# Expert rows turned by a transposing DMA instead of TensorE, a packed value projection, and a new planned order, in a kernel of attention and two mixtures

## The chip, the cores and the metric

The kernel runs on one core of a Trainium2 chip. The metric is device time in microseconds; the kernel before takes 529.66 us, the median of 3 runs (524.53 to 529.88). All engines of the core are named as in the profile: PE is TensorE, DVE is VectorE, ACT is ScalarE, POOL is GpSimd, SP is SyncE, whose only work here is to issue transfers.

## What is computed

Three stages follow each other, cut here to what matters:

```python
# 1: attention, 4 batches, 8 heads, 576 tokens, head size 64; heads 0-3 see the last 32 keys, heads 4-7 every fourth of 128
attn = softmax(where(mask, q @ k.T / 8, -1e9)) @ v
# 2: a mixture of 4 attention experts over x (4, 576, 512): all four are computed, the two best are kept
logits = x @ w_gate
y[e] = softmax(causal((x @ wq[e]) @ (x @ wk[e]).T / 8)) @ (x @ wv[e]) @ wo[e]
x2 = sum of w[kk] * y[topk[kk]]
# 3: a mixture of 8 feed-forward experts; each of the 2304 tokens goes to one expert
e = argmax(logits2) if s == 0 or local_gate < 0.5 else the expert of the token before
out = p[e] * (relu(x2 @ w1[e]) @ w2[e])       # w1: 512 x 1024, w2: 1024 x 512
```

The third stage is worked in float16 pairs: a value is kept as a high and a low part, and a product is the sum of high x high, high x low and low x high.

## The kernel before

The program has two parts.

**The planned part** holds the first two stages, the routing and three early slots of the third. Its instructions are recorded (class `Plan`), and `order` puts them in one order for each engine. It takes the instruction with the largest key that can start, where the key is the length of the chain behind the instruction, plus a number from the table `OFF` for the unit that it belongs to. So `OFF` sets the order. Its first units are these:

- `warm` filler matmuls (120, of `wn` = 256 columns) that write the tile Y from a tile of zeros. They have the lowest key and stand where PE has nothing else.
- `front` and `p1_stream`: the attention of eight pairs of heads (i = 0 to 7, two a batch). For a pair `p1_load` loads k and q, `p1_q` (POOL, ACT) lays q out, `p1_s` makes scores (PE, writes S) and their maximum (DVE), `p1_sub` and `p1_nrm` subtract and divide (POOL) around an exponential (ACT), `p1_t` transposes (PE, writes T) and `p1_pv` multiplies by v (PE, writes X and A). q is loaded into the tile of that pair's v, of which there are two, and v is loaded over it later by `p1_loadv`.
- `proj(b)`: the projections of batch b. q and k come first (matmuls of 288 columns into A), then v and the gate (line 417, as everything that is recorded): for each block of 128 tokens 12 matmuls of 260 columns, 256 for v and 4 for the gate. The fifth block has only 64 tokens and takes 12 matmuls too.
- `attn_stream`, `out_proj`, `route`, `early`, `slots`: the second stage's attention, its output, and the lists by which tokens go to experts.

**The slots.** The third stage works on groups of 128 tokens of one expert. `for t in range(NE, STATIC): slot(t, ...)` runs 18 of them in fixed program order, a conditional one follows; three early ones are in the planned part. One slot t is:

- SP: `w_load(t + 1)` (line 1237) issues eight loads of 512 KB into the staging tile `stg`, which are skipped where the expert stays the same. Each waits until DVE has split the chunk that lay there. SP's instructions stand in program order, so SP runs ahead of the engines by about a slot.
- POOL: `x_gather(t + 2)` (line 1266) gathers 128 rows of x2 by index from DRAM into one of `xgb` = 3 buffers, two slots ahead. At the slot's end `x_out(t)` (line 1312) scatters the 128 result rows. A buffer comes free when the slot's last ScalarE instruction (line 1309) has read its scale from it.
- ACT and DVE: eight `w_split` (lines 1257 and 1258) make the next slot's weights into high and low parts.
- PE: `mm1` twice (48 matmuls of 128 columns each, lines 1291 to 1293), then `x_t(t + 1)` (eight transposes of 128 x 128, line 1277, which ACT copies from PSUM, line 1279), then `mm2` (24 matmuls of 512 columns, lines 1303 to 1305).

Of the kernel before, what the change touches and what calls it, by code (L numbers as in the profile page):

```python
# [21 lines left out]
NB = 18  # L22
# [9 lines left out]
OFF = (20338.85, -10835.23, -17409.01, -12864.95, -10987.6, -10593.49, -17890.54, -11899.78, 22686.67, -19177.35,  # L32
# [27 lines left out]
KN = {"x0": (0, 1), "qk": (0, 1), "v2": (0, 1), "x2": (1, 1), "yt": (0, 1), "w": (0, 1), "f32t": 3,  # L60
      "early": 3, "pfl": (100000,), "wn": 256, "xp": "XA", "warm": 120, "off": OFF,
      "xgb": 3, "x2b": 3, "hx": "X", "hy": "A", "h2": "X", "fc": (0, 4),
      "banks": {"S": 2, "T": 2, "A": 2, "X": 1, "Y": 1}, "share": 32040, "emax": 22992,
# [95 lines left out]
class Plan:  # L159
# [96 lines left out]
    def price(eng, name, out, ins, a, k):  # L256
# [3 lines left out]
        if eng == "T":  # L260
            src = ins[-1] if name == "matmul" else ins[0]
            big = (src.proto if isinstance(src, View) else src).dtype == F32
            if sh[0] == 64 and n in (32, 64, 256, 288) and name == "matmul":
                return n / 2.4e3 * (2 if big else 0.5) + 0.003
# [175 lines left out]
def tile_attention_moe_moe(ctx: ExitStack, tc, qd, kd, vw, wqk, wvg, wo, woT, wg9, w1, w2,  # L440
# [77 lines left out]
    vh_w = wpool.tile([128, 4, 260], F16, name="wv_h")  # L518
    vl_w = wpool.tile([128, 4, 260], F16, name="wv_l")
    LDS, SPL, SVL, SE, TT, XP = {}, {}, {}, {}, {}, {}  # L520
    XH, XL = {}, {}

    S1 = [ld.tile([128, NB, 64], F32, name=f"s1{z}", bufs=1) for z in range(KN["bs"])]
    for y in S1:
        V.memset(y[:, :, 0:1], 1e-9)
    QZ = [ld.tile([128, 2 * NB, 64], F32, name=f"ldq{z}", bufs=1) for z in range(KN["bq"])]
    for z, y in enumerate(QZ):
        for h in range(2):
            (V if z else P).memset(y[64 * h:64 * h + 64, :, 32 - 32 * h:64 - 32 * h], 0.0)

    def p1_load(i):
        b, m = divmod(i, 2)
# [785 lines left out]
    def slot(t, hh, hl):  # L1318
# [15 lines left out]
        if nx:  # L1334
            x_t(t + 1)
# [174 lines left out]
```

## Time and profile before

| | |
|---|---|
| runs, us | 529.88, 529.66, 524.53 (median 529.66) |
| the profiled execution | 525.19 us, its span 523.3 us |
| PE, DVE, ACT, POOL busy in the span | 497.1, 427.2, 367.0, 137.0 us |
| planned part | 0 to 303.5 us |
| slots | 303.5 to 514 us, 19 of them |
| granted TensorE clock, mean | 0.987 of full speed |

Busy time is the time in which at least one instruction of an engine was under way; matmuls overlap, so the step from one start to the next is what a matmul costs its engine. The 9.3 us behind 514 us hold the last scatter and the program's end.

### The profile page before, as it was taken

What the parts mean: (1) busy time and instruction counts of PE and PEld (TensorE: products, weight loads), DVE (VectorE), ACT (ScalarE), POOL (GpSimd) and SP (SyncE); (2) the same over time, 40 slices, a digit from 0 to 9 for tenths busy, and PEclk for the clock granted to TensorE, in tenths of its full rate; (3) what the DMA queues carried; (4) which work ended last, traced back from release to release, by engine and by line L of the source; (5) the groups of instructions that cost most, each with busy time, mean ns of one, the idle gap of its engine ahead of it and who ended that gap; (6) DMA issues with size and microseconds to landing.
All of it is one profiled execution on the core that took longest, in us unless ns stands there. A gap on an engine that the chain in (4) does not pass through costs nothing.

```text
span 523.3 us, 17303 instructions
## 1 busy us (share of the span) xinstructions
PE 497.1 (95%) x6794; PEld 382.1 (73%) x6794; DVE 427.2 (82%) x1221; ACT 367.0 (70%) x620; POOL 137.0 (26%) x169
## 2 busy tenths in 40 slices
PE   7899999998999999989799999999999999999992
PEld 5787888887887887756577667777677776677760
DVE  4857558877988877899797169999999999999993
ACT  3454436664668657486482279999999999999992
POOL 7748233013321001131300211421112211123111
PEclk9999989999999999999999999999999999999997
DMA  8749777253203012312751826592165199561210
GB/s 310 277 135 283 223 221 208 60 195 118 67 25 72 26 46 64 90 70 55 254 210 53 320 104 211 189 329 86 42 212 192 49 358 381 175 216 60 63 43 15
DMA packets 33047, 79.89 MB, mean 153 GB/s; under 512 B 7486, under 2 KB 16190, under 8 KB 31936
## 3 DMA queue, kind: packets, MB, share of 16 engines
q1 hardware_dynamic: 29280, 67.70, 38.9%
q0 software_dynamic: 3680, 11.03, 6.1%
q8 instruction: 55, 0.90, 0.7%
q14 instruction: 32, 0.26, 0.2%
HBM read 112.52 MB, written 10.49 MB: 235 GB/s over the span
## 4 chain that ended last, share of the span: by engine, by line
DMA 20%; issue 19%; PE 11%; DVE 2%; POOL 0%; ACT 0%; POOLq 0%; another core or an unknown queue 0%
DMA out_dram<-o,SIDX 19%; PE A L417 3%; PE X L417 3%; DMA share<-x2d,GIDX 2%; PE T L417 1%; PE Y L417 1%; DVE s L417 1%; DVE tl L417 1%; DVE share L417 0%; PE S L1291 0%; PE S L1293 0%; PE S L1292 0%; PE A L1305 0%; PE A L1303 0%; PE A L1304 0%
## 5 line engine op out<-in xcount | busy, mean ns | idle before, releaser
L1258 DVE SCALAR_TENSOR_TENSOR share<-share 128x1024 f16<-128x1024 f32 x152 | 177.4, 1219 | 15.5 <-ACT share L1257 15.3
L1257 ACT ACTIVATE share<-share 128x1024 f16<-128x1024 f32 x152 | 149.7, 1048 | 0.2 <-DMA share<-in_w_dram 0.2
L417 PEld LDWEIGHTS <-share 128*128 128x128 f16 (+1 forms) x1430 | 116.9, 100 | 40.2 <-issue 4.2
L1293 PE MATMUL S<-share 128*128 128x128 f16 x608 | 102.8, 219 | 0.0
L1292 PE MATMUL S<-share 128*128 128x128 f16 x608 | 102.8, 219 | 0.0
L1291 PE MATMUL S<-share 128*128 128x128 f16 x608 | 102.8, 219 | 0.0
L417 PE MATMUL A<-share 128*128 128x288 f16 (+3 forms) x768 | 89.8, 270 | 0.7 <-DVE share L417 0.4
L1312 POOL DMA_INDIRECT out_dram<-o,SIDX x19 | 26.8, 1411 | 155.2 <-ACT o L1309 147.0
L1292 PEld LDWEIGHTS <-share 128*128 128x128 f16 x608 | 59.4, 98 | 2.3
L1291 PEld LDWEIGHTS <-share 128*128 128x128 f16 x608 | 59.5, 98 | 2.3
L1293 PEld LDWEIGHTS <-share 128*128 128x128 f16 x608 | 59.5, 98 | 0.0
L1303 PE MATMUL A<-share 128*128 128x512 f16 x152 | 57.8, 380 | 0.0
L1305 PE MATMUL A<-share 128*128 128x512 f16 x152 | 57.5, 378 | 0.0
L1304 PE MATMUL A<-share 128*128 128x512 f16 x152 | 57.5, 378 | 0.0
L417 ACT ACTIVATE th<-T 128x512 f16<-128x512 f32 (+3 forms) x84 | 42.0, 514 | 16.8 <-PE T L417 14.5
L417 ACT ACTIVATE s<-s,mx 128x256 f32<-128x256 f32 (+4 forms) x72 | 40.6, 582 | 13.9 <-DVE mx L417 12.8
L417 ACT ACTIVATE share<-A 128x288 f16<-128x288 f32 (+3 forms) x65 | 29.6, 455 | 21.5 <-PE A L417 14.0
L417 DVE CUSTOM_DVE_ANT_0 s<-S,tri 128x256 f32<-128x256 f32 (+4 forms) x80 | 37.1, 476 | 5.2 <-PE S L417 4.3
L417 ACT ACTIVATE share<-share 128x512 f16<-128x512 f32 (+4 forms) x52 | 27.2, 561 | 19.7 <-POOL share L417 11.5
L417 PE MATMUL S<-share 128*64 128x64 f32 (+5 forms) x672 | 37.7, 242 | 3.4 <-POOL share L417 2.0
L417 DVE SCALAR_TENSOR_TENSOR tl<-T,th 128x512 f16<-128x512 f32 (+2 forms) x60 | 35.2, 594 | 2.7 <-ACT th L417 2.3
L417 POOL TENSOR_TENSOR share<-f32t,share 128x512 f16<-128x512 f32 (+1 forms) x15 | 16.0, 1072 | 74.8 <-ACT f32t L417 40.8
(208 smaller groups left out, 935.8 us busy)
## 6 DMA issues: line engine op xcount, KB each, us to landing
share<-in_w_dram SPq DMA_DIRECT2D x160, 512.0 KB
share<-in_vw_dram SPq DMA_DIRECT2D x8, 1152.0 KB
share<-in_kd_dram SPq DMA_DIRECT2D x8, 608.0 KB
share<-in_qd_dram SPq DMA_DIRECT2D x8, 576.0 KB
x2d<-share SPq DMA_DIRECT2D x16, 256.0 KB
share<-qkhl SPq DMA_DIRECT2D x16, 144.0 KB
kk<-qkhl SPq DMA_DIRECT2D x16, 144.0 KB
share<-share SPq DMA_DIRECT2D x16, 72.0 KB
```

The costliest lines, as they stand in the source:

```text
L417: getattr(q, name)(*[bind(x) for x in a], **{n: bind(x) for n, x in k.items()})
L1257: A.activation(h, stg[:, c, :], AF.Copy, scale=64.0)
L1258: V.scalar_tensor_tensor(l, stg[:, c, :], 64.0, h, op0=OP.mult, op1=OP.subtract)
L1291: T.matmul(p[:, i, :], wh_[:, c], xt[:, d, :], start=(d == 0), stop=False)
L1292: T.matmul(p[:, i, :], wh_[:, c], xt[:, 4 + d, :], start=False, stop=False)
L1293: T.matmul(p[:, i, :], wl_[:, c], xt[:, d, :], start=False, stop=(d == 3))
L1303: T.matmul(p, hh[:, f, :], wh_[:, a], start=(f == 0), stop=False)
L1304: T.matmul(p, hh[:, f, :], wl_[:, a], start=False, stop=False)
L1305: T.matmul(p, hl[:, f, :], wh_[:, a], start=False, stop=(f == 7))
L1312: return nc.gpsimd.indirect_dma_start(out=orows, out_offset=bass.IndirectOffsetOnAxis(ap=SIDX[:, t:t + 1], axis=0), in_=o, in_offset=None, ...
```

## The change

In words, and then cut to the core:

1. In the slots the transposes leave PE and ACT. `x_t(t)` issues one transposing DMA from SP, from the gathered rows straight into one of three tiles `x3n`. It is issued inside `w_load`, behind the fifth of the eight weight loads. In the planned part (slots 0 to 3) `x_t` stays as it was. Gathers go out three slots ahead, into four buffers.
2. The value projection of a batch's last 64 tokens is packed: the columns of `wvg` are laid out as two halves of 132 (two experts and the gate, twice), and each half is a matmul of its own onto one half of the output partitions. The tiles behind it (vh, vl, th, tl, L) follow that layout, and the small DMA that copied the gate weights to the other 64 partitions falls away.
3. From the third pair on, q is loaded into a tile of its own (`XR`), not into v's.
4. 80 filler matmuls of 224 columns in the place of 120 of 256, and a new table `OFF`.

```diff
-OFF = (20338.85, -10835.23, -17409.01, -12864.95, -10987.6, -10593.49, -17890.54, -11899.78, 22686.67, -19177.35,
...
+OFF = (-16886.08, -14259.07, -16656.7, -12252.26, 20190.67, -13444.65, 19116.25, 11235.69, 18875.34, -17551.66,
...
-      "early": 3, "pfl": (100000,), "wn": 256, "xp": "XA", "warm": 120, "off": OFF,
-      "xgb": 3, "x2b": 3, "hx": "X", "hy": "A", "h2": "X", "fc": (0, 4),
+      "early": 3, "pfl": (100000,), "wn": 224, "xp": "XA", "warm": 80, "off": OFF,
+      "xgb": 4, "x2b": 3, "hx": "X", "hy": "A", "h2": "X", "fc": (0, 4),
...
+    XR = ld.tile([128, 2 * NB * 32], F32, name="ldx", bufs=1)
...
-        x = v.rearrange("p w e d -> p (w e d)")[:, :2 * NB * 32].rearrange("p (z j c) -> p z j c", z=2, j=NB)
+        x = v.rearrange("p w e d -> p (w e d)")[:, :2 * NB * 32] if i < 2 else XR
+        x = x.rearrange("p (z j c) -> p z j c", z=2, j=NB)
         SQ.dma_start(x, qd[b, m])
...
-            o = ps("A", [128, 260])
+            o = ps("A", [128, 264 if t < 4 else 132])
             for d in range(4):
...
+                for x, w, last in ((xh, vh_w, False), (xh, vl_w, False), (xl, vh_w, d == 3)):
+                    k = d == 0 and x is xh and w is vh_w
+                    if t < 4:
+                        T.matmul(o[:, :260], x[:, d, c], w[:, d, :260], start=k, stop=last)
+                        continue
+                    for z in range(2):
+                        T.matmul(o[64 * z:64 * z + 64], x[:, d, c], w[:, d, 132 * z:132 * z + 132], start=k, stop=last)
...
-        SQ.dma_start(W[64:128, 4, :], W[0:64, 4, :])
...
             w_regs(t)()
             for c in range(8):
                 w_dma(t, c)()
+                if c == 4:
+                    x_t(t)
             return
...
     def x_t(t):
         x = XG[t][:, :DM].bitcast(F16)
-        p = ps("T", [128, 512]).bitcast(F16).rearrange("p (a b) -> p a b", a=8) if REC[0] else P3T[t % 2]
+        if not REC[0]:
+            XT[t] = X3N[t % len(X3N)]
+            nc.sync.dma_start_transpose(out=XT[t], in_=x)
+            return
+        p = ps("T", [128, 512]).bitcast(F16).rearrange("p (a b) -> p a b", a=8)
...
-        if t + 2 < SLOTS:
-            x_gather(t + 2)
+        if t + 3 < SLOTS:
+            x_gather(t + 3)
...
-        if nx:
-            x_t(t + 1)
...
         if t == NE:
             x_gather(t + 1)
+            x_gather(t + 2)
             return
...
+    X3N = [p3.tile([128, 8, 128], F16, name=f"x3n_{i}", bufs=1) for i in range(3)]
```

The instructions stand in this order at three places. First SP in the slots, the loads of one slot, before:

```order
L1228 TENSOR_LOAD EXP_111
L1228 TENSOR_LOAD CHG_113
L1237 ISA
L1237 DMA share<-in_w_dram 128x1024
L1237 ISA
L1237 DMA share<-in_w_dram 128x1024
```

and in the changed kernel, from the fourth load of a slot on:

```order
L1253 ISA
L1253 DMA share<-in_w_dram 128x1024
L1253 ISA
L1253 DMA share<-in_w_dram 128x1024
L1295 DMA_TRANSPOSE x3n_5165<-share 128x8x128
L1253 ISA
L1253 DMA share<-in_w_dram 128x1024
```

Before, eight loads follow each other; now one more transfer, the transposing one, stands between the fifth and the sixth.

Second ACT in one slot, before:

```order
L1257 ACTIVATE share<-share 128x1024 x2
L1295 ACTIVATE share<-S_69 128x512
L1257 ACTIVATE share<-share 128x1024 x2
L1295 ACTIVATE share<-S_70 128x512
L1279 ACTIVATE share<-T_72 128x1024
L1257 ACTIVATE share<-share 128x1024 x4
L1309 ACTIVATE o_0_5151<-A_73,share 128x512
```

and in the changed kernel:

```order
L1275 ACTIVATE share<-share 128x1024 x2
L1317 ACTIVATE share<-S_69 128x512
L1275 ACTIVATE share<-share 128x1024 x2
L1317 ACTIVATE share<-S_70 128x512
L1275 ACTIVATE share<-share 128x1024 x4
L1331 ACTIVATE o_0_5160<-A_73,share 128x512
```

The copy from T is gone ahead of the last four splits; the eight transposes in the same place on PE are gone with it.

Third SP in the first microseconds, behind the first two pairs' k and q and the constants, before:

```order
L417 DMA share<-in_vw_dram 128x2304
L417 DMA share<-in_kd_dram 128x1216
L417 DMA share<-in_vw_dram 128x2304
L417 DMA share<-in_wqk_dram 128x512
L417 DMA share<-in_kd_dram 128x1216
L417 DMA share<-in_wqk_dram 128x512
L417 DMA share<-in_qd_dram 128x1152
```

and in the changed kernel:

```order
L416 DMA share<-in_qd_dram 128x1152
L416 DMA share<-in_vw_dram 128x2304
L416 DMA share<-in_kd_dram 128x1216
L416 DMA share<-in_vw_dram 128x2304
L416 DMA share<-in_wqk_dram 128x512
L416 DMA share<-in_kd_dram 128x1216
L416 DMA share<-in_wqk_dram 128x512
```

The third pair's q moved from behind the last weights of q and k to the front of the row.

## Rows read from the trace of the kernel before

**Rows 1.** Stretches: length, then busy us of PE, PEld, DVE, ACT, POOL; clock, DMA share, GB/s.

```profile
0.00:303.50 303.50, 287.54 (x4361) 227.69 (x4362) 228.27 (x1031) 169.30 (x391) 87.43 (x130) 0.99 0.47 148
303.50:514.00 210.50, 209.55 (x2434) 154.44 (x2432) 198.31 (x190) 197.70 (x229) 48.17 (x38) 1.00 0.47 165
```

**Rows 2.** Stretches: two single slots, and eighteen slots together.

```profile
392.97:403.98 11.01, 11.01 (x132) 8.13 (x129) 10.46 (x11) 10.49 (x13) 2.49 (x3) 1.00 0.59 214
425.99:437.00 11.01, 11.01 (x132) 8.13 (x129) 10.46 (x11) 10.38 (x13) 2.49 (x3) 1.00 1.02 391
...
316.40:514.00 197.60, 196.65 (x2278) 144.58 (x2275) 187.90 (x181) 186.02 (x216) 45.69 (x36) 1.00 0.49 173
```

**Rows 3.** PE in order of time, first third: start, length in us, what it writes.

```profile
19.84 1.05 PE L417 MATMUL Y<-share 128*128 128x256 f16 x8
20.72 0.54 PE L417 MATMUL T<-ident,share 128*128 128x128 f32 x3
...
32.45 1.16 PE L417 MATMUL Y<-share 128*128 128x256 f16 x9
33.53 0.92 PE L417 MATMUL S<-share 128*64 128x64 f32 x24
34.38 1.64 PE L417 MATMUL A<-share 128*128 128x288 f16 x12
```

**Rows 4.** All engines in order of time, the middle of one slot.

```profile
496.23 0.61 PE L1277 MATMUL T<-id,share 128*128 128x128 f16 x8
...
496.68 0.38 PE L1303 MATMUL A<-share 128*128 128x512 f16 x1
...
498.94 4.63 DVE L1258 SCALAR_TENSOR_TENSOR share<-share 128x1024 f16<-128x1024 f32 x4 [0.37 <-ACT share L1257]
```

**Rows 5.** Groups of instructions: count, busy us, mean ns, idle before.

```profile
L1279 ACT ACTIVATE share<-T 128x1024 f16<-128x1024 f16 x19 | 19.4, 1024 | 0.0
...
L1277 PE MATMUL T<-id,share 128*128 128x128 f16 x152 | 11.6, 219 | 0.0
```

**Rows 6.** DVE in order of time, where it waits for nothing.

```profile
323.36 6.90 DVE L1258 SCALAR_TENSOR_TENSOR share<-share 128x1024 f16<-128x1024 f32 x6 [0.33 <-ACT share L1257]
330.18 0.68 DVE L1296 SCALAR_TENSOR_TENSOR share<-S,share 128x512 f16<-128x512 f32 x1
330.78 2.35 DVE L1258 SCALAR_TENSOR_TENSOR share<-share 128x1024 f16<-128x1024 f32 x2
```

**Rows 7.** A stretch of the planned part.

```profile
91.60:104.70 13.10, 13.10 (x263) 10.70 (x261) 11.62 (x42) 9.08 (x23) 1.21 (x2) 1.00 0.26 60
```

**Rows 8.** POOL in order of time; below, its transfers with count and us to landing.

```profile
337.94 1.41 POOL L1312 DMA_INDIRECT out_dram<-o,SIDX  x1 [6.81 <-ACT o L1309]
339.65 1.08 POOL L1266 DMA_INDIRECT share<-x2d,GIDX  x1 [0.30 <-PE S L1293]
...
share<-x2d,GIDX POOLq DMA_INDIRECT x24, 4.8
```

**Rows 9.** What SP waited for in the slots: us, times, longest.

```profile
SPq L1237 <- DVE share L1258: 122.3, 133, 13.2
```

**Rows 10.** PE in order of time: value projection and output projection of 64 rows.

```profile
214.86 1.52 PE L417 MATMUL A<-share 128*64 128x260 f16 x12
...
279.49 0.28 PE L417 MATMUL A<-wo_l,yth 128*64 128x256 f16 x2
279.60 0.28 PE L417 MATMUL A<-wo_h,ytl 128*64 128x256 f16 x2
```

**Rows 11.** SP and POOL in order of time: the third pair's q.

```profile
25.72 0.33 SPq L417 DMA_DIRECT2D share<-in_qd_dram  x1
...
29.74 3.46 POOL L417 COPY share<-share 64x192 f32<-64x192 f32 x8 [3.74 <-DMA share<-in_qd_dram]
```

**Rows 12.** Two stretches of the planned part.

```profile
66.00:72.00 6.00, 6.00 (x137) 5.47 (x134) 3.50 (x31) 1.30 (x4) 0.00 (x0) 0.74 0.83 281
...
240.00:260.00 20.00, 15.33 (x221) 11.88 (x220) 17.26 (x82) 11.14 (x24) 4.91 (x5) 1.00 0.47 157
```

More of the change, by code (lines that the diff above doesn't have):

```diff
@@ L31 @@
 XW = DM + 1
-OFF = (20338.85, -10835.23, -17409.01, -12864.95, -10987.6, -10593.49, -17890.54, -11899.78, 22686.67, -19177.35,
[27 rows of a table removed]
+OFF = (-16886.08, -14259.07, -16656.7, -12252.26, 20190.67, -13444.65, 19116.25, 11235.69, 18875.34, -17551.66,
[26 rows of a table added]
 KN = {"x0": (0, 1), "qk": (0, 1), "v2": (0, 1), "x2": (1, 1), "yt": (0, 1), "w": (0, 1), "f32t": 3,
-      "early": 3, "pfl": (100000,), "wn": 256, "xp": "XA", "warm": 120, "off": OFF,
-      "xgb": 3, "x2b": 3, "hx": "X", "hy": "A", "h2": "X", "fc": (0, 4),
-      "banks": {"S": 2, "T": 2, "A": 2, "X": 1, "Y": 1}, "share": 32040, "emax": 22992,
+      "early": 3, "pfl": (100000,), "wn": 224, "xp": "XA", "warm": 80, "off": OFF,
+      "xgb": 4, "x2b": 3, "hx": "X", "hy": "A", "h2": "X", "fc": (0, 4),
+      "banks": {"S": 2, "T": 2, "A": 2, "X": 1, "Y": 1}, "share": 32740, "emax": 23840,
       "lay": (0.1, 3088, 4624, 5400), "cp": 1.0, "peek": 0.0, "pp1": (-23, -8, 0, 0), "ppr": (-27,),
@@ L262, in price @@
             big = (src.proto if isinstance(src, View) else src).dtype == F32
-            if sh[0] == 64 and n in (32, 64, 256, 288) and name == "matmul":
+            if sh[0] == 64 and n in (32, 64, 132, 256, 288) and name == "matmul":
                 return n / 2.4e3 * (2 if big else 0.5) + 0.003
@@ L517, in tile_attention_moe_moe @@
     wl = wpool.tile([128, 4, 512], F16, name="wqk_l")
-    vh_w = wpool.tile([128, 4, 260], F16, name="wv_h")
-    vl_w = wpool.tile([128, 4, 260], F16, name="wv_l")
+    vh_w = wpool.tile([128, 4, 264], F16, name="wv_h")
+    vl_w = wpool.tile([128, 4, 264], F16, name="wv_l")
     LDS, SPL, SVL, SE, TT, XP = {}, {}, {}, {}, {}, {}
@@ L523, in tile_attention_moe_moe @@
     S1 = [ld.tile([128, NB, 64], F32, name=f"s1{z}", bufs=1) for z in range(KN["bs"])]
+    zero = share[:, 32628:32740].bitcast(F16)
+    V.memset(zero, 0.0)
     for y in S1:
         V.memset(y[:, :, 0:1], 1e-9)
+    XR = ld.tile([128, 2 * NB * 32], F32, name="ldx", bufs=1)
     QZ = [ld.tile([128, 2 * NB, 64], F32, name=f"ldq{z}", bufs=1) for z in range(KN["bq"])]
@@ L705, in prep @@
         for d in range(4):
-            split(stage(wvg[d], 260), vh_w[:, d], vl_w[:, d], 256.0)
+            split(stage(wvg[d], 264), vh_w[:, d], vl_w[:, d], 256.0)
             yield 0
@@ L728, in tile_attention_moe_moe @@
         for t in sm.reserve([128, 5, 128], F16, x, 3):
-            P.memset(t[64:128, 4, :], 0.0)
+            P.memset(t[:, 4, :], 0.0)
     YT = {}
@@ L766, in proj @@
         if b < 2:
-            P.memset(vh[64:128, 4], 0.0)
-            P.memset(vl[64:128, 4], 0.0)
-        P.memset(vh[:, :, :, 64:65], 512.0)
-        P.memset(vl[:, :, :, 64:65], 0.0)
+            P.memset(vh[:, :, :, 64:65], 512.0)
+            P.memset(vl[:, :, :, 64:65], 0.0)
+            for h in range(2):
+                P.memset(vh[64 * h:64 * h + 64, 4, 2 - 2 * h:4 - 2 * h], 0.0)
+                P.memset(vl[64 * h:64 * h + 64, 4, 2 - 2 * h:4 - 2 * h], 0.0)
         L = tiny.tile([128, NT, E1], F32, name="L", bufs=2)
-        P.memset(L[64:128, 4, :], 0.0)
@@ L773, in proj @@
         for t in range(NT):
-            n = 128 if t < 4 else 64
-            o = ps("A", [128, 260])
+            o = ps("A", [128, 264 if t < 4 else 132])
             for d in range(4):
-                c = slice(128 * t, 128 * t + n)
-                T.matmul(o[:n], xh[:, d, c], vh_w[:, d, :], start=(d == 0), stop=False)
-                T.matmul(o[:n], xh[:, d, c], vl_w[:, d, :], start=False, stop=False)
-                T.matmul(o[:n], xl[:, d, c], vh_w[:, d, :], start=False, stop=(d == 3))
@@ L781, in proj @@
-            ov = o[:n, :256].rearrange("p (e d) -> p e d", e=4)
-            split(ov, vh[:n, t, :, 0:64], vl[:n, t, :, 0:64], 2.0 ** -9, "v2")
-            A.activation(L[:n, t, :], o[:n, 256:260], AF.Copy, scale=float(2.0 ** -18))
+                c = slice(128 * t, min(S, 128 * t + 128))
+                for x, w, last in ((xh, vh_w, False), (xh, vl_w, False), (xl, vh_w, d == 3)):
[5 more added lines that the diff above has]
+                        T.matmul(o[64 * z:64 * z + 64], x[:, d, c], w[:, d, 132 * z:132 * z + 132], start=k, stop=last)
@@ new lines, in proj @@
+            if t < 4:
+                r = lambda x: x[:, t].rearrange("p (a e) d -> p a e d", a=2)[:, :, :, 0:64]
+                ov = o.rearrange("p (a b) -> p a b", a=2)[:, :, :128].rearrange("p a (e d) -> p a e d", e=2)
+                split(ov, r(vh), r(vl), 2.0 ** -9, "v2")
+            else:
+                for z in range(2):
+                    r = slice(64 * z, 64 * z + 64)
+                    split(o[r, :128].rearrange("p (e d) -> p e d", e=2), vh[r, 4, 2 * z:2 * z + 2, 0:64],
+                          vl[r, 4, 2 * z:2 * z + 2, 0:64], 2.0 ** -9, "v2")
@@ L784, in proj @@
+            A.activation(L[:, t, :], o[:, 128:132], AF.Copy, scale=float(2.0 ** -18))
             yield 1.33
@@ L865, in at_b @@
             tp = ps("T", [128, 4, 128])
-            T.transpose(tp[:64, 0, :], s[:, 512:576], ident)
-            split(tp[:64, 0], th[:64, 4], tl[:64, 4], 4096.0)
+            if es[0] == 0:
+                T.transpose(tp[:64, 0, :], s[:, 512:576], ident)
+            else:
+                T.transpose(tp[:, 0, :], s[:, 448:576], ident)
+            r = slice(32 * es[0], 32 * es[0] + 64)
+            split(tp[r, 0], th[r, 4], tl[r, 4], 4096.0)
         UB[u] = (th, tl)
@@ L1372, in run @@
         plan.next()
-    zero = share[:, 31784:32040].bitcast(F16)
-    V.memset(zero, 0.0)
     wp = ps("Y", [128, 512])
@@ L1409, in tile_attention_moe_moe @@
     P3A = BANKS["A"][:2]
-    P3T = [BANKS['T'][_].bitcast(F16).rearrange('p (a b) -> p a b', a=8) for _ in range(2)]
+    X3N = [p3.tile([128, 8, 128], F16, name=f"x3n_{i}", bufs=1) for i in range(3)]
     for t in range(NE, STATIC):
@@ L1449, in layout @@
     wqk = cat([i["moe_wq"][e] for e in range(E1)] + [i["moe_wk"][e] for e in range(E1)], axis=1)
-    wvg = cat([i["moe_wv"][e] for e in range(E1)] + [i["moe_w_gate"]], axis=1)
+    wv, g = i["moe_wv"], i["moe_w_gate"]
+    wvg = cat([wv[0], wv[1], g, wv[2], wv[3], g], axis=1)
     wo = i["moe_wo"].reshape(2, 128, DM)
```

53 rows, old and new, of the table OFF are left out of this document.

## The prediction, made before the changed kernel ran

> **What bounds the kernel now.** I read the stretches of the trace first, then the order of time inside one slot, then who waits for whom. The program has two parts. Up to 303.5 us runs the planned part (attention, the first mixture, routing, three early slots), in an order that a planner fixed; from there to 514 us run 19 slots of the second mixture, one like the other [rows 1]. In the slots TensorE leaves nothing: the slot from 392.97 to 403.98 us is 11.01 us long and PE is busy for 11.01 of them, VectorE for 10.46, ScalarE for 10.49 [rows 2]. So a slot is as long as PE's work in it, with VectorE half a microsecond behind as the next bound. In the planned part PE is busy for 287.5 of 303.5 us, and part of that is filler (the matmuls that write Y from a zero tile): from 19.84 to 33.5 us seven groups, 60 fillers, take 7.7 us together, the first and the last of them in [rows 3]. There PE waits for others and fills the time.
>
> **The slots: eight transposes go from PE, one copy from ScalarE.** In a slot the eight transposes start at 496.23 and the next matmul on the path (line 1303) at 496.68: they hold PE for 0.45 us [rows 4]. The groups say that it is so in every slot: 152 transposes and 19 copies, eight and one for each of 19 slots [rows 5]. Nothing hides them, since PE has no gap there. The new slot is 11.01 - 0.45 = 10.56 us, if nobody else needs more.
>
> VectorE at its own pace: six low-part splits from 323.36 to 330.18, 1.14 us each, and 0.60 us from an h split to the next instruction [rows 6]; 8 x 1.14 + 2 x 0.60 = 10.3 us, under 10.56. Its longest wait in a slot, 0.37 us before the last four splits, is for the ScalarE split that stands behind the copy of 1.02 us [rows 4, 5]; with the copy gone ScalarE has 10.49 - 1.02 = 9.5 us of work in 10.56. So PE still ends last, and the term is 19 x 0.45 = **8.5 us**. From below it is bounded by a VectorE that keeps 0.5 us of waits (10.8 us a slot, 19 x 0.2 = 4 us); more than 8.5 us it cannot be.
>
> By the Trainium skill ("TensorE: Matmul & The Clock Gate", Part 4) a transpose of 128 x 128 in a kernel costs about 275 ns; an estimate from that is 19 x 8 x 0.275 = 42 us for this term. The trace disagrees: in a row they follow each other every 0.056 us (0.45 / 8), and the 0.22 us of the group's mean is how long one is under way, not what it costs the next.
>
> **What the transposing DMA costs.** The trace has none. It moves 256 KB from SBUF to SBUF. Its time on the rings lies between 0.67 us (256 KB at 391 GB/s, the fullest slot [rows 2]) and 1.1 us (the row with the poorest ratio of bytes to busy share, 60 GB/s at a share of 0.26 [rows 7]); the farthest bound is the landing of a gather of the same size, 4.8 us from issue [rows 8], if all of that were ring time. I take 1 us. Over the slots the rings are busy for a share of 0.49, so 0.51 x 11 = 5.6 us a slot are free [rows 2].
> By the skill ("DMA: Bandwidth & Descriptors", Latency and other measured facts) such a DMA runs at 261 GB/s, an estimate of 1.0 us; no run here shows it, and the sum would be the same.
>
> The issue stands on SP's queue behind the fifth weight load and ahead of the last three. SP waited 122.3 us in the slots for VectorE to free the staging tile [rows 9], 6.4 us a slot, so the time in which SP issues one more DMA is hidden while it stays under that. What the DMA itself waits for is old by then: SP gets to it for slot t+1 when VectorE has split the fifth chunk of slot t, about the middle of slot t-1, and the gather of slot t+1 was issued at the start of slot t-2's work, because gathers now go out three slots ahead into four buffers (a gather follows the scatter that frees its buffer by 1.7 us and lands 4.8 us after its issue [rows 8]). That leaves some 9 us of slack. Its result is needed at the start of slot t+1, some 16 us after SP gets there. The three weight loads behind it are needed about a slot later. So it costs 0 on the path; without that cover it would cost its landing time in each slot.
>
> The first slot is tighter: the DMA for the second slot waits for a gather that goes out only after the slot table is known. Its buffer is no longer shared with the second early slot, so it follows the gather before it at once; I price this at nothing, with 1 us as a bound.
>
> **The packed value projection.** The last 64 rows of a batch took twelve matmuls of 260 columns, 1.52 us with the last one's tail, some 0.11 us each [rows 10]. Now there are 24 of 132 columns, in pairs on the two halves of the array. The output projection has such pairs already, of 256 columns, and a pair advances in 0.11 us (279.49 to 279.60 [rows 10]); 132 columns then take 0.057, twelve pairs 0.7 us instead of 1.35. Four batches: **2.6 us**, all PE time. The additional small splits on ScalarE and VectorE (one of each a batch), the cleared tiles, and the small weight copy on SP that falls away lie beside other work: VectorE has 75 us of idle time in this part (228 of 303.5 busy [rows 1]).
>
> **The new order and the third pair's q.** In the order of before the third head pair's q could only be loaded when the first pair's v was used up: issued at 25.72 us, GpSimd waited for it until 29.74, and its scores began at 33.53 [rows 11, 3]. Meanwhile PE filled 7.7 us. Now q has its own buffer, and its load stands ahead of the first v load. On PE all 80 fillers stand ahead of the second group of transposes, and two groups of scores and two of transposes more than before stand ahead of the first projection matmul (line of 34.38 us). Scores advance 0.85 us a group (33.53 to 34.38), a transpose group about 0.4 [rows 3]: 2 x 0.85 + 2 x 0.4 = 2.5 us of real work in the place of fillers. The bounds: 0 (the place of the 60 fillers is simply idle) and 7.7 us (all is filled by real work). I take **5.0**: the 2.5 that the order shows and half of the other 5.2, because the third pair's whole chain on VectorE and GpSimd moves ahead with its q. Later idle time of PE (4.7 us from 240 to 260 us is the largest piece [rows 12]) may grow or shrink under the new order by some 4 us; I take 0.
>
> **Sum.** 8.5 + 2.6 + 5.0 = 16.1 us. The profiled execution took 525.19 us (span 523.3): 525.2 - 16.1 = 509.1. The median of before, 529.66, stands 4.5 us above that execution, the lowest run 0.7 below it; I place the median of the changed kernel halfway, at 509.1 + 2.4 = 511.5.
>
> **Rivals.**
> *The order gives nothing (0.18).* The fillers are gone and their place is idle, and TensorE's clock falls. For it: chains of that part end on VectorE and GpSimd, not on PE. In the one early stretch where the clock fell, 66 to 72 us, the mean granted clock was 0.74 [rows 12], which loses 0.26 x 6 = 1.6 us; two more such are 3.2. Then 525.2 - 8.5 - 2.6 + 3.2 = 517.3, with the half step 519.7.
> *The transposes cost PE more than their step (0.02).* If each cost more than 0.056 us, through a change of mode around them that the step hides, the slot would fall to VectorE's 10.3 us and the slots give 19 x 0.7 = 13.5: 504.1, with the half step 506.5. Against it: matmul, transposes and matmul follow each other without a gap in [rows 4]. The skill's 275 ns ("TensorE: Matmul & The Clock Gate", Part 4) would mean this one.
> *VectorE becomes the bound of the slots (0.10).* Against it the 10.3 us above; for it that waits of 0.5 us a slot may stay with another releaser. The slots then give 4, not 8.5: 513.6, with the half step 516.
> *Slower: the transposing DMA crowds the weight loads (0.07).* In the slot from 425.99 the rings were full (share 1.02 [rows 2]): a whole expert was loaded. If the DMA holds the rings for more than the 5.6 us that a slot leaves free, each microsecond more costs 19; at 8 us it is 2.4 x 19 = 46 us: 509.1 + 46 = 555. Against it: 5.6 us for 256 KB is 47 GB/s, a fifth of the poorest row.
> The rule behind this one is the skill's ("DMA: Bandwidth & Descriptors", Issuing engines are not separate DMA queues): all transfers share the same 16 engines and interleave.
>
> **How the numbers follow.** Forecast 0.63, rivals as given. Low end: all 7.7 us of filler saved and 4 us of idle less, 509.1 - 2.7 - 4 = 502.4, rounded to 503. High end: the first rival with the whole 4.5 us between profile and median, 517.3 + 4.5 = 521.8, rounded to 521. That leaves out the third rival and some of the tails, under 0.2; the forecast's own range is 505 to 517. One per cent is about what a measurement of this kernel can tell from no change: faster by more means under 524.4. The forecast (0.61 of its 0.63), the costlier transposes (0.02), the first rival mostly (0.13) and the second (0.08) end there: 0.84; 0.08 within 1%, 0.08 slower.
>
> **What would show it.** Scatters (line 1312 of before) 10.56 us apart; no PE instruction that writes T in a slot; VectorE with under 0.3 us idle in a slot; the DMA's landing well before the first matmul of its slot, and no ScalarE split that waits for a weight load. The first projection matmul of 288 columns before 32 us, and the first slot's matmul at about 296 us instead of 303.8. I am wrong if slots stay near 11 us, or if PE's idle time before 60 us grows by what the fillers gave up.

## The result, and the profile after

| | before | changed |
|---|---|---|
| median of 20 runs each, same chip | 526.74 us | 530.66 us |
| lowest, highest | 523.92, 530.2 | 523.76, 538.28 |
| profiled execution | 525.19 us (span 523.3) | 529.74 us (span 527.9) |
| first slot's scatter issued at | 316.43 us | 317.81 us |
| the 18 slot periods behind it | 197.6 us | 203.45 us |

The ratio is 1.0051, 95% interval [1.0026, 1.0076]: half a per cent slower, which counts as within 1%. Ratios leave out runs that are over 1.5% above the kernel's fastest, a slower state of the chip; e4 below has only two others, 530.71 and 533.43 us, and so no ratio. Forecast were 511.5 us and a range of 503 to 521; both were wrong. The two profiled spans differ by 4.6 us: 1.4 in the planned part, 5.85 in the slots, and -2.6 at the end: before, the span ended 9.3 us behind the last scatter's issue, now 6.6. The 1.4 us are not clear of noise: in the nine profiled runs below and here that have this planned part unchanged, the first scatter is issued between 316.6 and 322.5 us. The slot periods repeat better: 203.45 here, 202.96 in e2, which has the same slots.

Stretches of the changed kernel (start:end, length, busy us of PE, PEld, DVE, ACT, POOL, clock, DMA share, GB/s): the planned part, the 18 slot periods, then single slots.

```profile
0.00:303.50 303.50, 279.92 (x4362) 221.34 (x4363) 225.82 (x1035) 170.89 (x395) 88.06 (x127) 0.99 0.47 150
317.81:521.26 203.45, 192.76 (x2133) 136.52 (x2130) 187.07 (x181) 169.30 (x198) 76.90 (x36) 0.98 0.65 189
327.80:340.77 12.97, 12.97 (x168) 10.14 (x165) 11.02 (x11) 9.67 (x12) 6.57 (x2) 1.00 1.01 279
...
393.15:406.76 13.61, 13.61 (x178) 10.78 (x176) 10.87 (x11) 9.66 (x12) 2.49 (x2) 1.00 0.96 260
438.87:456.72 17.85, 14.31 (x179) 10.54 (x176) 10.99 (x11) 10.11 (x12) 2.69 (x3) 1.00 1.05 243
...
489.64:500.18 10.54, 10.54 (x124) 7.70 (x121) 10.54 (x11) 9.44 (x12) 6.57 (x2) 1.00 0.34 80
```

The last row is a slot as forecast (10.56): PE leaves nothing, and the rings (the core's 16 DMA engines, whose mean busy share is the last but one number) are a third busy. The three above it are late, and in each the rings are full, yet they move only 243 to 279 GB/s where a full slot of before moved 391 [rows 2]. Against 18 x 10.54 = 189.7 us the slots lose 13.7 us; this sum is called the excess below. In the planned part PE is busy 7.6 us less than in [rows 1] and the time is not shorter: what PE no longer does became idle time.

What engines waited for in the slots (us, times, longest):

```profile
ACT share L1275 <- DMA share<-in_w_dram: 17.8, 17, 2.8
...
PEld L1327 <- DVE share L1318: 10.1, 12, 1.5
...
PEld L1325 <- ACT share L1317: 6.5, 4, 4.1
```

ScalarE's high-part split (line 1275, 1257 before) waits for weight loads, 17.8 us in all; before it waited 0.2 us for them. PE then waits for what ScalarE and VectorE pass on. The transposing DMA's issue on SP (its 19 in a row: shortest, median and longest in ns, first and last start), and SP's order in the latest slots:

```profile
L1295 SPq DMA_TRANSPOSE x3n<-share x19: 1246/1259/4792, 291.5 to 508.2; - x19
...
425.18 2.20 SPq L1295 DMA_TRANSPOSE x3n<-share  x1
427.75 7.60 SPq L1253 DMA_DIRECT2D share<-in_w_dram  x8
435.46 4.79 SPq L1295 DMA_TRANSPOSE x3n<-share  x1
```

And two stretches amid the latest slot, behind the DMA issued at 435.46; below them one of before, amid a reload:

```profile
443.00:445.00 2.00, 1.88 (x9) 0.90 (x10) 1.02 (x2) 1.79 (x2) 0.00 (x0) 1.00 2.06 95
445.00:447.00 2.00, 1.06 (x5) 0.11 (x2) 1.96 (x3) 0.85 (x3) 0.00 (x0) 1.00 0.68 89
```

```profile
434.00:436.00 2.00, 2.00 (x13) 0.93 (x11) 2.00 (x3) 1.70 (x2) 0.00 (x0) 1.00 1.02 416
```

For 4 us the rings moved some 92 GB/s, a quarter of what they moved in a reload before. (In a share over 1 the times of packets overlap.) Nearly all packets of these 4 us, 818 of 857, are under 512 B, as those of the transposing DMA are; so for that time the reload hardly moves:

```profile
DMA packets 857, 0.37 MB, mean 92 GB/s; under 512 B 818, under 2 KB 818, under 8 KB 857
```

Theory: the transposing DMA takes the rings from the expert reloads. There are six reloads in the slots (before: 173 GB/s over 197.6 us is 34.2 MB [rows 2]; a slot without reload moves 0.55 MB, 18 of them 9.9; the rest is 5.8 times 4.19 MB). Rivals: the hold on SP's queue, the gathers three ahead, the new planned part.

### The profile page after: what moved, and what is told of

It is laid out like the page before. It is cut to its first block, busy times and chain, and to the rows that moved or that the text cites. A ratio compares the mean times of both kernels' runs of the same rounds, so it can differ in the third digit from the quotient of the medians.

```text
span 527.9 us, 17027 instructions
## 1 busy us (share of the span) xinstructions
PE 486.9 (92%) x6650; PEld 368.0 (70%) x6650; DVE 423.8 (80%) x1225; ACT 351.0 (66%) x605; POOL 169.3 (32%) x166
## 4 chain that ended last, share of the span: by engine, by line
PE 39%; DVE 18%; DMA 17%; issue 16%; POOL 4%; ACT 4%; SPq 0%; POOLq 0%; ACTq 0%; DVEq 0%
PE A L416 16%; DMA out_dram<-o,SIDX 8%; DMA share<-in_w_dram 6%; PE T L416 6%; PE S L416 5%; DVE share L1276 5%; PE Y L416 4%; PE X L416 4%; DVE share L416 4%; POOL share L416 3%; DMA share<-x2d,GIDX 3%; DVE tl L416 2%; ACT share L1275 2%; DVE s L416 1%; PE S L1315 1%
## 5 line engine op out<-in xcount | busy, mean ns | idle before, releaser
L1276 DVE SCALAR_TENSOR_TENSOR share<-share 128x1024 f16<-128x1024 f32 x152 | 177.7, 1216 | 21.7 <-ACT share L1275 20.7
L1275 ACT ACTIVATE share<-share 128x1024 f16<-128x1024 f32 x152 | 151.4, 1049 | 18.7 <-DMA share<-in_w_dram 17.8
L416 PEld LDWEIGHTS <-share 128*128 128x128 f16 (+1 forms) x1438 | 111.9, 100 | 41.6 <-issue 4.6
L1314 PE MATMUL S<-x3n,share 128*128 128x128 f16 x576 | 97.4, 219 | 0.0
L1315 PE MATMUL S<-x3n,share 128*128 128x128 f16 x576 | 97.4, 219 | 0.0
L1313 PE MATMUL S<-x3n,share 128*128 128x128 f16 x576 | 97.4, 219 | 0.0
L416 PE MATMUL A<-share 128*128 128x288 f16 (+3 forms) x816 | 88.2, 266 | 1.2 <-ACT L L416 0.8
L1334 POOL DMA_INDIRECT out_dram<-o,SIDX x19 | 46.4, 2440 | 129.6 <-ACT o L1331 115.2
L1325 PE MATMUL A<-share 128*128 128x512 f16 x152 | 58.6, 386 | 5.4 <-ACT share L1317 5.4
L1327 PE MATMUL A<-share 128*128 128x512 f16 x152 | 58.5, 385 | 4.3 <-DVE share L1318 3.8
L1326 PE MATMUL A<-share 128*128 128x512 f16 x152 | 58.6, 386 | 0.0
L416 POOL TENSOR_TENSOR share<-f32t,share 128x512 f16<-128x512 f32 (+1 forms) x15 | 16.1, 1074 | 110.5 <-ACT f32t L416 106.2
L416 ACT ACTIVATE share<-A 128x288 f16<-128x288 f32 (+3 forms) x67 | 29.9, 447 | 26.9 <-PE A L416 21.4
L1284 POOL DMA_INDIRECT share<-x2d,GIDX x25 | 39.8, 1594 | 12.6 <-issue 7.0
L416 PE MATMUL S<-share 128*64 128x64 f32 (+5 forms) x672 | 36.4, 236 | 2.4 <-POOL share L416 1.1
L416 DVE SCALAR_TENSOR_TENSOR share<-A,share 128x288 f16<-128x288 f32 (+3 forms) x52 | 24.1, 464 | 17.3 <-ACT share L416 16.7
```

The source lines that it names most:

```text
L416: getattr(q, name)(*[bind(x) for x in a], **{n: bind(x) for n, x in k.items()})
L1275: A.activation(h, stg[:, c, :], AF.Copy, scale=64.0)
L1276: V.scalar_tensor_tensor(l, stg[:, c, :], 64.0, h, op0=OP.mult, op1=OP.subtract)
L1284: return nc.gpsimd.indirect_dma_start(out=x, out_offset=None, in_=x2d[:LB * S] if t < NE else x2d, in_offset=bass.IndirectOffsetOnAxis(ap= ...
L1313: T.matmul(p[:, i, :], wh_[:, c], xt[:, d, :], start=(d == 0), stop=False)
L1314: T.matmul(p[:, i, :], wh_[:, c], xt[:, 4 + d, :], start=False, stop=False)
```

## The experiments

Times are medians, ratios are to the kernel before on the same chip. The 18 periods run from the first slot's scatter to the last.

| run | us | ratio [95%] | 18 periods |
|---|---|---|---|
| changed kernel | 530.66 | 1.0051 [1.0026, 1.0076] | 203.5 |
| e1, turned by TensorE | 525.74 | 0.9981 [0.9948, 1.0014] | 196.8 |
| e2, only the transposing DMA | 531.6 | 1.0077 [1.004, 1.0115] | 203.0 |
| e3, no reloads | 514.07 | 0.9747 [0.9679, 0.9814] | 189.2 |
| e4, behind the eighth load | 536.16 | none | 207.7 |
| e5, plain copy | 520.73 | 0.9893 [0.9852, 0.9934] | 191.1 |
| e6, twice | 536.49 | 1.0183 [1.0122, 1.0245] | 211.1 |
| e15, two halves | 533.12 | 1.0124 [1.0086, 1.0161] | 202.0 |
| e9, from ScalarE | 570.46 | 1.0864 [1.0804, 1.0925] | 239.1 |
| e11, from ScalarE, two ahead | 552.2 | 1.0528 [1.0475, 1.058] | 215.9 |
| e8, 60 fillers fewer | 527.85 | 1.0017 [0.9986, 1.0047] | 197.5 |
| e10, more PE work, old order | 534.78 | 1.0173 [1.0123, 1.0223] | 197.2 |
| e12, more PE work, new order | 531.19 | 1.0069 [1.0028, 1.0111] | 196.8 |
| e7, packed alone | 541.14 | 1.0269 [1.0232, 1.0305] | 197.2 |

**Is it the transposing DMA, and only beside reloads? (e1, e2, e3)**

```diff
 e1, from the changed kernel:
-                if c == 4:
-                    x_t(t)
...
-            nc.sync.dma_start_transpose(out=XT[t], in_=x)
...
+        if nx:
+            x_t(t + 1)
         sp_(4, 5)
 e2, from the kernel before, the reverse, with "xgb": 4, "share": 32740 (room for the buffers) and gathers three ahead
 e3, from the changed kernel:
-                w_dma(t, c)()
```

> The changed kernel with the slots' transposes back on TensorE and their copy on ScalarE, between mm1 and the last four splits as before; planned part, four buffers and gathers three slots ahead stay as changed. Theory: the transposing DMA takes ring time away from the expert reloads, and that is the whole lateness in the slots. Then every slot is 11.01 us again, no ScalarE split waits for a weight load, 18 slot periods take 198 us and not 203.5, and the kernel stands at about 530.7 - 5.3 = 525. Rival: the late slots come from the gathers three ahead or from the planned part (which SP's loads or POOL's gathers begin late). Then they stay, each 0.45 us longer than now, and the kernel stands at 530 to 539.

> The kernel before with the transposing DMA in the slots, four buffers and gathers three ahead, and nothing else of the change: the planned part is that of before, instruction by instruction on TensorE. Theory: the slots lose what they lose in the changed kernel, 203.5 against 197.6 us for 18 periods, so 526.7 + 5.9 = 532.6. Rival: the loss came from the new planned part that hands the slots a different start; then all slots are 10.56 us and the kernel stands at 526.7 - 8.5 = 518.

> The changed kernel without the weight loads of the slots: SP issues only the transposing DMA, and the splits work on what lies in the staging tile (the result is therefore not the reference's; all arithmetic stays). Theory of the rings: with no reload to crowd, every slot is 10.54 us; 18 periods take 189.8 us instead of 203.5, and the kernel stands at 530.7 - 13.7 = 517. Rival: VectorE or PE sets 10.54 only on average and the late slots are made by POOL's stretched gathers or by the transposing DMA landing late; then some slots stay over 11 us and the kernel stays above 523.

All three came out as the theory has it. With TensorE's transposes the slots are 11.0 us again although the gathers stay three ahead. With the transposing DMA alone, on the planned part of before, the same slots are late (among them 12.85, 11.45, 13.59 and, the largest, 17.79 us). Without reloads not one is:

```profile
316.58:505.76 189.18, 188.18 (x2133) 136.95 (x2130) 186.51 (x181) 169.38 (x198) 52.52 (x37) 1.00 0.28 69
```

18 periods in 189.18 us are 17 of 10.54 and one of 10.0. So the step that takes eight transposes from PE works as forecast, and loses only where a reload is under way.

**Bytes, packets, or the place in SP's queue? (e4, e5, e6, e15)**

```diff
 e4:
-                if c == 4:
+                if c == 7:
 e5:
-            nc.sync.dma_start_transpose(out=XT[t], in_=x)
+            nc.sync.dma_start(XT[t].rearrange("p a b -> p (a b)"), x)
 e6, behind the transposing DMA:
+            nc.sync.dma_start_transpose(out=XD[t % 2], in_=x)
 e15, behind the third and the sixth load:
+            nc.sync.dma_start_transpose(out=XT[t][:, 4 * half:4 * half + 4], in_=x[:, 512 * half:512 * half + 512])
```

> The changed kernel with the transposing DMA issued behind the eighth weight load of a slot instead of behind the fifth. Theory of the rings: its ring time is the same and it collides with the same reload, so the kernel stays within 3 us of 530.7 and the late slots are late by about 13.7 us together. Rival, SP's queue: the issue (1.25 us, up to 4.8 us) holds the three loads behind it, which are the last of a reload; without that the late slots lose at least half of their excess, and the kernel falls to 524 or less.

> The changed kernel with a plain copy of the same 256 KB, SBUF to SBUF, in the place of each transposing DMA of the slots (rows of 2 KB; the tile is not turned, so the result is not the reference's, and the work on the engines is the same). In the kernel without reloads every slot was 10.54 us, so the lateness needs the weight loads; open is whether the extra bytes do it or the 1024 packets of 256 B and the 1.25 to 4.8 us for which SP issues them. Theory of the packets: 256 KB in long rows take 0.7 us of ring time and about 0.3 us of SP; the late slots lose two thirds or more of their 13.7 us, and the kernel stands at 520 to 522. Rival, the bytes: any 256 KB more in a full ring cost the same; the kernel stays at 528 to 532.

> The changed kernel with each transposing DMA of the slots issued twice, the second into a tile that nobody reads. Theory of the rings: without a reload a slot stays at 10.54 us, and the excess of the slots with reloads about doubles, from 13.7 to some 27 us: 544. Rival, only the landing of the turned tile matters (or the place in SP's queue): the second one adds at most its issue time behind the fifth load, and the kernel stays under 536.

> The changed kernel with each transposing DMA of a slot cut into two of 128 KB (four of the eight blocks each), issued from SP behind the third and behind the sixth weight load. Theory of the packets: as many packets of 256 B beside the same reload, so the excess of the slots with reloads stays at 10 to 18 us and the kernel at 527 to 534. Rival, the burst: what hurts is that 1024 descriptors at once fill the queue (up to 4.8 us of issue) and stop the rings for 3 to 4 us; halves fit, the excess falls under 7 us and the kernel to 524 or less.

Issue rows on SP, of e5 and of e15, as above:

```profile
L1295 SPq DMA_DIRECT2D x3n<-share x19: 470/472/788, 294.2 to 497.8; - x19
```

```profile
L1295 SPq DMA_TRANSPOSE x3n<-share x38: 1189/1208/2200, 293.4 to 512.6; - x38
```

The page's row of SP's transfers (packets, MB, share of 16 engines over the span), in e1, which has the same planned part and no DMA for the tile, changed, and with the plain copy; below them that of e3 from 301 to 303 us, where one transposing DMA runs and no reload:

```profile
q1 hardware_dynamic: 28960, 67.71, 38.5%
```

```profile
q1 hardware_dynamic: 49024, 72.69, 45.3%
```

```profile
q1 hardware_dynamic: 31696, 72.69, 41.4%
```

```profile
q1 hardware_dynamic: 1056, 0.26, 68.1%
```

The plain copy moves the same 4.98 MB in 2736 packets instead of 20064, and its excess is 1.4 us, not 13.7. So it is not the bytes. Ring time of one transfer, in the mean of the 19: (0.453 x 527.9 - 0.385 x 523.4) / 19 = 1.98 us turned, (0.414 x 517.4 - 0.385 x 523.4) / 19 = 0.67 us plain. The turned mean mixes two kinds: where no reload is under way one takes 0.681 x 2 = 1.4 us. In e3's list of packets 18 of the 19 transposing DMAs have none over 0.14 us and take 1.4 us from first to last; in the changed kernel the one amid the latest slot has packets of up to 2.9 us and takes 5.3.

Issued twice, the excess grows to 21.4 us. That is 7.7 us more, 1.3 for each of six reloads, about one more issue (1.25 us), and the kernel's 536.49 us met neither expectation (544, or under 536); e6 decides little. Behind the eighth load the excess is 18.0: ScalarE still waits 15.1 us for weight loads, and now PE waits 12.7 us for the turned tile too; the place is not the cause. In two halves the excess is 12.3: it is no burst. The halves also hold SP longer, 45.7 us in sum from 300 us on in the place of 28.7, and the slots are no later, so SP's issue time is not what costs either. (As a whole e15 is 0.7% slower than the changed kernel by the ratios; its first scatter is issued 4.7 us later in the profile, ahead of all slot periods. Why is not known.)

What of the transfer costs, its small packets or the turning itself, is not shown: a plain copy in packets of 256 B was not run.

The Trainium skill ("Advanced Engine Details and Errata", X-Bar Transpose (TRN2)) says that transposing DMAs are as fast as regular ones. Here they are not, by 1.4 us with no reload beside it to 0.67, and the measurement decides.

**Another queue, and more time (e9, e11)**

```diff
 e9, from the changed kernel:
-                if c == 4:
-                    x_t(t)
...
-            nc.sync.dma_start_transpose(out=XT[t], in_=x)
+            nc.scalar.dma_start_transpose(out=XT[t], in_=x)
...
+        if nx:
+            x_t(t + 1)
         sp_(4, 5)
 e11, in the place of the last:
+        for n in (NE + 1, NE + 2) if t == NE else (t + 2,):
+            if n < SLOTS:
+                x_t(n)
```

> The changed kernel with the slots' transposing DMA issued from ScalarE, between mm1 and the last four splits (where the copy from PSUM stood before), instead of from SP amid the weight loads. The ring time is the same, SP's weight loads are no longer held by an issue of 1.25 to 4.8 us; ScalarE has 9.4 us of work in a slot and gets 1.25 us more, 10.65. Theory of the rings (packets that share them with the reload): the late slots stay, with the excess of 10 us and more over 18 periods, plus up to 2 us for a ScalarE at 10.65; 530 to 535. Rival, the hold on SP's queue: the weight loads go out in time, the excess falls under 5 us, and the kernel stands at 520 to 525.

> The changed kernel with the transposing DMA issued from ScalarE as in the run before this one, but two slots ahead of its use instead of one (the first slot issues two). From ScalarE, one slot ahead, the weight loads were in time (4.4 us of waits for them in all the slots) and all slots without a reload were 10.54 us, but beside a reload the turned tile took some 13.7 us from issue to use, 8.5 us more than it had, once for each of six reloads. Theory: the transposing DMA's 1024 small packets take turns with the reload's long ones, so it needs some 14 us beside a reload, whoever issues it; with 15.6 us of time it is hidden, the slots go to 10.54 to 10.9 us each (190 to 196 us for 18), and the kernel stands at 516 to 523, faster than both kernels. Rival: the rings have no room for it at all in a reload; then the lateness only moves to the weight loads or to the next transposing DMA, and the excess stays at 10 us and more: 528 or higher.

From ScalarE's queue the loads come in time and the turned tile is late instead. Its issue for one of the late slots, and PE's first matmul on it (idle before it, and what ended that):

```profile
407.94 1.25 ACTq L1293 DMA_TRANSPOSE x3n<-share  x1
```

```profile
421.60 0.26 PE L1311 MATMUL S<-x3n,share 128*128 128x128 f16 x1 [8.52 <-DMA x3n<-share]
```

13.7 us from issue to use; six slots, one for each reload, take 12.7 to 20.7 us, and the others 10.5 (the first 9.9). At 570.46 us the run lies far above both expectations (530 to 535, 520 to 525): I had not reckoned with the late tile. I had then taken from this that the DMA only needs more time. It fell too: two slots ahead, nobody waits for the tile, and the loads are late again. Waits of e9 and of e11 (us, times, longest):

```profile
PE S L1311 <- DMA x3n<-share: 37.5, 7, 8.5
...
ACT share L1273 <- DMA share<-in_w_dram: 4.4, 6, 0.8
```

```profile
ACT share L1273 <- DMA share<-in_w_dram: 30.5, 25, 7.3
```

One of the two is late in every arrangement that was tried: a reload and a turned tile did not fit beside each other. That transfers share the rings whichever engine issues them is the Trainium skill's rule ("DMA: Bandwidth & Descriptors", Issuing engines are not separate DMA queues); both runs agree in that the two still collide. But the queue decided which of them was late, and by how much: 18 periods of 239.1 and 215.9 us against 203.5. Why the rings move so little while the two meet (92 GB/s above) stays open.

**The planned part (e8, e10, e12, e7)**

```diff
 e8, in Plan.issue of the kernel before, behind the order:
+                if name == "matmul" and self.ops[i].unit == 0:
+                    fill += 1
+                    if fill > 60:
+                        continue
 e10 in the kernel before, e12 in e1 (132 in the place of 260):
+                if name == "matmul" and k.get("start") and a[0].shape[0] == 64 and a[0].shape[-1] == 260:
+                    for _ in range(24):
+                        getattr(q, name)(*[bind(x) for x in a], start=True, stop=True)
 e7: the kernel before with part 2 of the change (the packing), and nothing else
```

> The kernel before with the same order on every engine, except that the last 60 of the 120 filler matmuls are not issued: those that stand on PE from 19.84 to 33.5 us and take 7.7 us there. Theory: their place is waiting time for chains on other engines, so nothing behind them comes earlier, and the kernel stays within 2 us of before (a clock that falls for lack of work costs 1 to 3 us). The prediction had priced that place at 5 us of gain (bounds 0 and 7.7): if PE sets the time there, the kernel falls to 520 to 522.

> The kernel before with the same order, and 24 more matmuls of 260 columns in front of the fifth block of every batch's value projection (overwritten by the block itself): 96 x 0.11 = 10.6 us of PE work at the place where the packing took 2.6 us away. If PE's work there sets the time, as the prediction had it, the kernel is 10 us slower, 537. Theory now: the planned part is a mesh of chains and PE's work there is worth only a part of itself; under 5 us slower.

> The changed kernel with the transposes back on TensorE (525.7 us), and 192 more matmuls of 132 columns in front of the fifth blocks of the value projection, overwritten by the blocks themselves: 192 x 0.055 = 10.6 us of PE work, as much as in the run on the kernel before (there 7.9 us slower, 0.75 for each microsecond). If a microsecond of PE work in the projections is worth as much in the new order, this run is 8 us slower than without it, 533.5, and the packing brought about 2 us, which the rest of the planned part (order, q, fillers) then lost again. Rival: the new order waits there anyway, the additional work is worth under 4 us (under 530), and the packing brought less than 1 us.

> The kernel before with the packed value projection alone (its table of numbers and everything else as before; the planner shifts some instructions, since its costs see the packing). From the slope of the run with more PE work (7.9 us for 10.6, 0.75) the 2.6 us that the packing saves on PE should be worth 2 us: a ratio of 0.996. Rival: the planned part gives all of it back as idle time, as it did with the fillers' place; ratio 1.000, or above it where the shifted order costs more.

The stretch from 20 to 40 us, before, with 60 fillers fewer, and in the changed kernel:

```profile
20.00:40.00 20.00, 19.27 (x462) 15.88 (x460) 13.35 (x63) 9.19 (x24) 11.79 (x23) 1.00 0.45 148
```

```profile
20.00:40.00 20.00, 15.07 (x360) 12.29 (x360) 11.51 (x52) 7.80 (x19) 10.15 (x17) 0.67 0.47 152
```

```profile
20.00:40.00 20.00, 15.66 (x421) 12.85 (x420) 14.83 (x76) 11.02 (x27) 14.92 (x27) 1.00 0.75 261
```

Without its fillers PE is busy 4.2 us less there and the granted clock falls to 0.67, and the kernel is 0.9 us slower [-0.7, 2.5]. What the slower clock costs can hide a gain here: at the reckoning of the prediction's first rival it is 0.33 x 20 = 6.6 us, an estimate from the row above. So e8 alone does not show that the fillers' place was waiting time. The changed kernel shows part of it: there the clock stays at 1.00 and PE is idle for 4.3 us of the same stretch, where before it was idle for 0.7.

10.6 us more of PE work cost 9.1 us by the ratio (7.9 by the medians) in the order of before, where I had expected under 5; the prediction's 10 was nearer. In the new order they cost 4.6 us (+-2.8; 0.88% of 527), between the two expectations. If a microsecond saved is worth as much as one added, which no run shows, the 2.6 us that the packing saves are worth 1.1 to 2.2 us, an estimate from these two slopes (0.43 and 0.86), nearer 1.1 in the new order. The packing alone, under the old table, is 14.3 us slower, where 2 us faster was expected. In its last stretch the clock is at 0.76 and PE has 8 us of idle time, while one of GpSimd's gathers waits 22.9 us, by the trace for a weight load:

```profile
260.00:303.50 43.50, 35.32 (x355) 24.27 (x356) 26.69 (x86) 16.92 (x30) 5.55 (x6) 0.76 0.65 233
```

```profile
POOL share L1279 <- DMA share<-in_w_dram: 22.9, 1, 22.9
```

The table was found for the program without the packing, and the packing shifts the order; so this run prices no packing, and the two can't be taken apart by it.

## Why the prediction was wrong, point by point

**Eight transposes and a copy leave the engines: right.** 10.54 us a slot without reloads (forecast 10.56); VectorE kept up.

**"So it costs 0 on the path": the step that failed.** It rested on "over the slots the rings are busy for a share of 0.49, so 5.6 us a slot are free". That is a mean over two kinds of slot. Of the 18 of before seven stand at 0.10 to 0.17, one of them below (1.8 us busy), and eleven, with a reload or part of one, at 0.55 to 1.02:

```profile
481.02:492.03 11.01, 11.01 (x132) 8.13 (x130) 10.46 (x11) 10.38 (x13) 2.48 (x2) 1.00 0.16 50
```

In the one kind 9 us are free; amid a reload (1.02 in the stretch from 434 us, above, and in [rows 2] itself) nothing is, and the DMA goes out in both. It took back 13.7 us of excess where 19 x 0.45 = 8.5 were gained: e2 gives the net, +4.1 us (0.77% of 527).

**Its size: 1 us taken, 0.67 to 1.1 as bounds.** Where no reload was under way it measured 1.4 us, outside of them: both bounds were rates of plain transfers, and the plain copy, 0.67, lies at the lower one. That alone would not have hurt a quiet slot. With a transfer that costs as little as that copy, the kernel stands at 520.7, just inside the range. Beside a reload the transposing DMA costs more than this ring time: 13.7 us over six reloads are 2.3 each, above 1.4.

**The issue, hidden under SP's 6.4 us: right in its effect.** It takes 1.25 us and up to 4.79, but e9 and e15 show that the hold is not what costs.

**Packed value projection, 2.6 us: right as PE work, too large as time.** The pairs advance as forecast; 24 of them are under way for 0.88 us, where 12 took 1.52 [rows 10]:

```profile
145.74 0.88 PE L416 MATMUL A<-share 128*64 128x132 f16 x24
```

That row is of e1. A microsecond of PE work added there cost 0.4 to 0.9 us, not one; what else bounds the part is not shown.

**The new order, 5.0 us: wrong, its lower bound 0 was right.** The first projection matmul came at 34.04 us, not before 32:

```profile
33.33 0.88 PE L416 MATMUL T<-ident,share 128*128 128x128 f32 x6
34.04 3.10 PE L416 MATMUL A<-share 128*128 128x288 f16 x24
```

Real work did move ahead of it, as the order showed, but it left idle time around it (4.3 us) instead of filling it: PE growing idle there was the prediction's own sign of being wrong. The first slot's matmul came at 305.31 us, not about 296 (303.76 before). By e1, packing, order, q and fillers together gained 1.0 us [-0.7, 2.7], where 7.6 were forecast; with the packing's estimate taken off, nothing that can be told from zero is left for the rest. What the order lost in which place stays open.

**The rivals.** Two came true together: "the order gives nothing" (0.18) for the planned part, though without its two falls of the clock, and "the DMA crowds the weight loads" (0.07) in the slots. The second named the right collision and the wrong condition: it was to begin at 5.6 us of ring time, by the same mean. I had priced them apart; together they end within 1%, which had 0.08.

**The sum.** 16.1 us of gain were forecast, a loss of 2.7 [1.4, 4.0] was measured. By runs: +4.1 for the DMA (e2) and -1.0 for the planned part (e1) give 3.1. Two slips in the prediction's sums change nothing in this: halfway from 525.19 to 529.66 is 2.2 us, not 2.4, and 502.4 and 521.8 were rounded inward to 503 and 521.

Of all variants e1 is the fastest with the full result, and not to be told from the kernel before. With this DMA the gain of 0.45 us a slot was only to be had where no reload is under way, which the routing decides while the kernel runs.

## What to carry over

Read a resource's free time in the stage where it is fullest, not as a mean: a transfer added to every turn of a loop is paid in the turns that already fill the rings. Measure a transfer in a new form, alone and beside the heaviest traffic, before pricing it by its bytes; a run with a plain copy in its place tells whether the bytes are what costs. And before idle-time fillers are counted as time to be won, take some away and read the granted clock with the time: if nothing gets faster at the same clock, something else owns that time; if the clock falls, as in e8, the run leaves it open.

## What was not expected of the hardware

- A transposing DMA took SP about 1.2 us to issue at both sizes tried: 1.25 us for 256 KB, 1.21 for 128 KB; the plain copy of 256 KB 0.47.
- GpSimd's scatter and gather grew from 1.41 and 1.12 us in the mean to 2.44 and 1.59. They are long where VectorE has no gap meanwhile, as the first two rows, and short where it waits, as the last two (POOL in order of time, changed kernel):

```profile
427.22 4.05 POOL L1334 DMA_INDIRECT out_dram<-o,SIDX  x1 [3.41 <-DMA share<-in_w_dram]
431.58 2.52 POOL L1284 DMA_INDIRECT share<-x2d,GIDX  x1 [0.31 <-issue]
...
456.72 1.30 POOL L1334 DMA_INDIRECT out_dram<-o,SIDX  x1 [14.85 <-ACT o L1331]
458.32 1.17 POOL L1284 DMA_INDIRECT share<-x2d,GIDX  x1 [0.30 <-issue]
```

  Nobody waited for them longer than the slot gives. That VectorE's work is the cause was not tried.
- Without 60 fillers (e8) the granted clock was at 0.50, the lower of its two levels (1.2 GHz), from 28 to 40 us, behind two microseconds in which PE did next to nothing:

```profile
24.00:26.00 2.00, 0.03 (x4) 0.04 (x4) 1.87 (x9) 1.12 (x3) 1.23 (x2) 1.00 0.49 146
26.00:28.00 2.00, 2.00 (x75) 1.94 (x76) 0.35 (x3) 0.45 (x2) 0.82 (x1) 0.68 0.27 46
28.00:30.00 2.00, 1.91 (x8) 1.11 (x6) 0.81 (x2) 1.71 (x5) 0.00 (x0) 0.50 0.66 251
```

  It stayed there while PE was busy again (2.00 of 2 us from 34 to 40). The kernel as a whole is at most 2.5 us slower; what the clock alone cost is not told apart.
